# Fewer filling multiplications at the start of a linear attention and MLP kernel, low words of the weights on ScalarE, and a new order of its work

## The chip, the cores and the metric

The kernel runs on one core of one Trainium2 chip. The metric is the device time of one execution in microseconds (us). TensorE multiplies matrices into PSUM; VectorE, ScalarE and GpSimd work on elements; SyncE issues nearly all the transfers. Each engine takes its own instructions strictly in the order in which the program lists them.

## The reference

The first part is a recurrence over 768 time steps for 4 batches and 8 heads of dimension 48. Its output, 3072 tokens of 384 numbers, goes through an MLP with an ELU:

```python
for t in range(S):                       # S = 768
    cur = einsum('bhd,bhe->bhde', u * k[t], v[t])
    y[:, :, t] = einsum('bhd,bhde->bhe', r[t], state + cur)
    state = w[t][..., None] * state + einsum('bhd,bhe->bhde', k[t], v[t])
x = y as (3072, 384)
h = x @ w_in                             # 384 x 2048
g = where(h > 0, h, exp(min(h, 0)) - 1)
out = g @ w_out                          # 2048 x 384
```

Inputs are float32 but the two MLP weights, which come as float64.

## The kernel before

**Attention.** The sequence is cut into 6 stages of 128 steps, and each stage into 4 *units* (24 in all, numbered from 0). The first four units take one batch each with a chunk of 128 steps, the others two batches with a chunk of 64. A unit needs on VectorE two scans over the decays w (`es`, `gs`), a product of the hats with k and r (`rh`), and a mask (`mk`); on TensorE the scores (`s`, with the transposes of k) and the values and state update (`v`); on ScalarE copies out of PSUM (`kt`, `xf`, `xh`). The diagonal of the scores, with the bonus u, comes for units 0 to 3 from a product `rkc` on VectorE, four small matmuls `pd` on TensorE (line 475), a copy `md` and eight spreading copies `sp` on ScalarE (line 485). For later units GpSimd makes two products (`rk`, `rku`, lines 458 and 461) and VectorE or GpSimd spreads. The mask `mk` (line 540) needs both the scores and the spread diagonal, and `v` needs the mask.

**MLP.** A stage has 512 tokens and 16 steps, one for each 128 of the 2048 hidden columns: `g1` multiplies into `ph`, `r1`, `r2`, `stt` make the ELU, `g2` adds into three accumulators. In stage 0 the first six steps run in two halves of 256 tokens, the first half as soon as units 0 and 1 are done, with plain float32 weights (lines 259 and 291). Other steps split both factors into a high and a low part (`gh`, `gl`, `w_h`, `w_l`) and use three matmuls for each (lines 263 and 294).

**Weights.** Each of the 16 tiles of weights is loaded as raw 64-bit words (line 606, `raw`). It is turned into float32 by `a` on ScalarE (line 611, scaling the high words), `cs` (`conv_low`, shifting the low words: line 616 on ScalarE or 618 on VectorE, by the table `LOW`), and two VectorE passes `cb` and `cc` (lines 626 and 630). For the split, `wh` (line 633) rounds and `wl` (line 645) subtracts. There are four raw buffers at first and later two; a tile's buffer comes free with `cc`.

**Order.** A planner with a table of assumed durations (`COST`), buffer counts (`SLOTS`) and due times lists all tasks once for all engines. Among the ready tasks of an engine it takes the one with the smallest due time plus its entry in `NUDGE`, which is keyed by the kind of task and its number. `RAW_AT` gives the earliest time of the plan at which the raw tiles 0, and 1 and later, may be issued. Ahead of a task with an entry in `FILL` the emitted program has that many multiplications of a matrix of ones with itself, 128 x 128 in float32 (`warm`, line 410). Their product is never read. The plan doesn't know of them.

Of the kernel before, what the change touches and what calls it, by code (L numbers as in the profile page):

```python
# [38 lines left out]
CUT = 384  # L39
K32 = 6  # L40
SIGN_ACT = ()
LOW = ['DVE']*2+['ACT']*14
RAWS = ["raw0", "raw1", "x1a", "x1b"] * 2 + ["raw0", "raw1"] * 4
DUE = {0: 9.0}
FILL = {("pd", 0): 29, ("s", 0): 12, ("v", 0): 1, ("pd", 1): 5, ("v", 1): 2, ("pd", 2): 7, ("s", 2): 5, ("g1", 0): 12}


def _pieces():
    res = []
    for h in range(H):  # L50
        s, e = h * D, (h + 1) * D
        while s < e:
# [22 lines left out]
FIRST = "ACT"  # L75
SPARE = (1,)
PAD = 32
RAW_AT = (1.6, 4.0)
LEAD = 69.5
DIAG = ['PE']*4+['POOL']*20  # L80
SPREAD = ["ACT"] * 4 + ["DVE"] * 4 + ["POOL"] * 16
# [2 lines left out]

LEADS = dict(ld="ld_w ld_k ld_v ld_rk ld_wx", es="es gs", rh="rkc rh kh pc sc", sp="rk rku md pd sp", fl="fl", s="s mk kt", v="v xf xh xl up", raw="raw", a="a",
             cc="cand cs cb cc cx sg", wl="wh wl wt", g1="g1 r1 r2 stt", g2="g2 gh gl")
NUDGE = dict(cc={0: 5, 2: 19.5, 4: 15.75, 5: -13.25, 14: 4.25},
             es={3: 11.5, 5: -23.75, 7: 1, 11: -42.5, 17: -5.25, 20: 12.75, 21: 40.5},
             g1={16: -3.5, 19: -3.5, 20: 4.25, 23: 5.75, 29: -7.5, 30: -8.25, 31: -13.25, 33: 21, 38: -15.75, 40: -29.75, 42: -33.75, 44: -17.5, 48: -70.75, 51: 26.75, 55: 44, 56: -10.5, 58: -10, 68: 34, 82: -8, 83: 12.5, 84: 6, 93: -7.5},
             g2={2: 6.75, 3: 26.5, 10: 1.5, 19: -1.75, 25: 0.25, 27: 2.25, 30: 0.75, 31: 14.75, 32: -6.5, 35: 9, 37: -11.25, 43: 28.5, 46: -25.25, 51: 8.5, 58: -13, 64: 2.25, 65: 14.5, 71: -25.5, 85: 6.5, 93: 1.75},  # L90
             ld={2: -16, 13: -16.5, 21: -36.75},
             raw={0: -6.75, 1: -6},
             rh={1: 10.25, 4: -3.75, 9: -18.75, 14: 23.5, 16: -14},
             s={4: -29.75, 9: -2.25, 12: -30.25, 13: 5, 21: 8.5},
             sp={4: -19.25, 5: 8.75, 9: 39.5, 13: 29.5, 17: -6.5},
             v={2: -5.5, 15: -2, 17: 6.75, 18: 24, 20: 22.25})
KIND = {n: k for k, v in LEADS.items() for n in v.split()}


class Plan:  # L100
# [5 lines left out]
    def add(self, key, eng, dur, fn, after=(), due=None, start=0.0, lock=False, size=0):  # L106
        self.tasks[key] = dict(key=key, eng=eng, dur=dur, fn=fn, after=list(after), due=due, start=start, lock=lock, size=size,
                               nudge=NUDGE.get(KIND.get(key[0]), {}).get(key[1] if len(key) > 1 else 0, 0.0))

# [212 lines left out]
def rwkv_elu_kernel(ctx, tc, wkr, rk, vp, u, uz, gkrw, gv, gu, wraw, out):  # L322
# [84 lines left out]
    def warm(n):  # L407
        pw = spare()[2][:, 0:P]
        for _ in range(n):
            nc.tensor.matmul(pw, ones, ones, start=True, stop=True)  # L410
# [193 lines left out]
    def load_w(f):  # L604
        raws[f] = raw_tile(f), None
        nc.sync.dma_start(raws[f][0].rearrange("p i k c -> p (i k c)"), wraw[f].bitcast(U32))

    def conv_a(f):
        g = w_f[f].bitcast(U32) if f < K32 else stg.tile([P, 2, NK, P], U32, tag="wg", name="wg", bufs=SLOTS["wg"])
        raws[f] = raws[f][0], g  # L610
        act(g.bitcast(F32), raws[f][0][:, :, :, 1::2].bitcast(F32), AF.Copy, scale=2.0 ** -112)  # L611

    def conv_low(f):
        w0 = raws[f][0][:, :, :, 0::2]
        if LOW[f] == "ACT":
            act(w0, w0, AF.Copy, bias=7.5 * 2.0 ** -10 - 0.5, scale=2.0 ** -29 - 2.0 ** -39)
        else:
            nc.vector.tensor_scalar(out=w0, in0=w0, scalar1=29, scalar2=None, op0=ALU.logical_shift_right)
# [106 lines left out]
    for f in range(NF):  # L725
        add(("raw", f), "SP", DMA_ISSUE, lambda f=f: load_w(f), start=RAW_AT[min(f, 1)], size=694)
        add(("a", f), "ACT", K["a"], lambda f=f: conv_a(f), [("raw", f)])
        e = LOW[f]
        add(("cs", f), e, K["la" if e == "ACT" else "cand"], lambda f=f: conv_low(f), [("raw", f)], lock=e == "DVE")
# [105 lines left out]
    with tc.manual_schedule():  # L835
        for t in plan.order():
            warm(FILL.get(t["key"], 0))
            t["fn"]()
# [137 lines left out]
```

## Time and profile before

| | us |
|---|---|
| median of 3 runs | 518.42 |
| lowest and highest run | 518.3, 519.65 |
| the profiled execution's own time | 517.97 |
| its span, first to last instruction | 515.8 |
| busy in the span: TensorE | 506.8 (98%) |
| busy: VectorE | 335.4 (65%) |
| busy: ScalarE | 270.6 (52%) |
| busy: GpSimd | 97.1 (19%) |

In the profile PE is TensorE, PEld its weight loads, DVE VectorE, ACT ScalarE, POOL GpSimd and SP SyncE. L410 is line 410 of the kernel. Names such as `am<-upper,pa` are the tile written and the tiles read. Ends of matmuls are modelled, so neighbouring ones overlap in the rows and a busy TensorE need not be at its peak. A float32 matmul leaves two records.

### The profile page before, as it was taken

The numbers are of one execution on the slowest core, as the hardware profiler recorded it, in microseconds if no ns is written. First come the engines' busy times: TensorE is split into PE (matmuls) and PEld (weight loads), VectorE is DVE, ScalarE is ACT, GpSimd is POOL, SyncE is SP. The second block draws the span as 40 slices with busy tenths as digits, with TensorE's granted clock in tenths as the row PEclk, the third lists the DMA queues.
The fourth block names the chain that finished last, engine by engine and source line by source line (L and its number), as shares of the span: only waits on it lengthen the run. The fifth ranks groups of instructions, "written<-read, shape, count | busy, mean of one in ns | idle before, by whom it ended". The sixth has DMA issues, their size and how long they took to land.

```text
span 515.8 us, 13882 instructions
## 1 busy us (share of the span) xinstructions
PE 506.8 (98%) x6070; PEld 417.8 (81%) x6070; DVE 335.4 (65%) x469; ACT 270.6 (52%) x520; POOL 97.1 (19%) x94
## 2 busy tenths in 40 slices
PE   9999999999999999999999999999999999999995
PEld 9998787787888888888788888887888877888884
DVE  6789999999589643498743487842499642423242
ACT  2779667657655344565545564443545443535351
POOL 2000123103455100264100174400161100000000
PEclk9999999999999999999999999999999999999998
DMA  8936944600843000856200674202332000010001
GB/s 258 337 132 201 319 139 142 189 3 4 260 117 106 3 3 3 243 154 160 57 19 3 197 204 143 75 0 79 99 101 56 22 1 3 0 62 0 1 1 66
DMA packets 18882, 51.09 MB, mean 99 GB/s; under 512 B 2304, under 2 KB 2688, under 8 KB 18816
## 3 DMA queue, kind: packets, MB, share of 16 engines
q1 hardware_dynamic: 18672, 50.08, 32.0%
q8 instruction: 49, 0.80, 0.6%
q14 instruction: 17, 0.14, 0.1%
q10 hardware_dynamic: 144, 0.07, 0.0%
HBM read 45.42 MB, written 4.72 MB: 97 GB/s over the span
## 4 chain that ended last, share of the span: by engine, by line
PE 86%; DVE 5%; ACT 3%; DMA 2%; issue 2%; POOL 0%; DVEq 0%; ACTq 0%; SPq 0%; POOLq 0%
PE ph L263 33%; PE acc L294 33%; PE pa L503 6%; PE acc L410 4%; PE pa L528 3%; PE pa L568 2%; PE ph L259 2%; PE acc L291 2%; PE pb L516 1%; DMA wx<-in_wkr_dram 1%; DMA wraw<-in_wraw_dram 1%; DVE m L273 1%; ACT m L270 1%; DVE wg L626 1%; ACT wg L611 1%
## 5 line engine op out<-in xcount | busy, mean ns | idle before, releaser
L273 DVE SCALAR_TENSOR_TENSOR m<-m,ph 128x512 f32<-128x512 f32 (+1 forms) x102 | 66.3, 651 | 98.3 <-ACT m L270 98.0
L267 ACT ACTIVATE m<-ph 128x512 f32<-128x512 f32 (+1 forms) x102 | 58.2, 571 | 108.7 <-PE ph L263 97.0
L263 PE MATMUL ph<-xh,w_l 128*128 128x512 f32 x270 | 105.4, 390 | 0.0
L294 PE MATMUL acc<-gh,w_l 128*128 128x512 f32 x268 | 104.6, 390 | 0.0
L281 DVE TENSOR_TENSOR gl<-m,gh 128x512 fp32r<-128x512 f32 x90 | 65.2, 726 | 39.4 <-ACT gh L277 39.3
L277 ACT CAST gh<-m 128x512 fp32r<-128x512 f32 x90 | 55.7, 619 | 59.4 <-PE acc L294 30.5
L294 PE MATMUL acc<-gh,w_h 128*128 128x512 f32 x180 | 71.9, 399 | 0.0
L263 PE MATMUL ph<-xh,w_h 128*128 128x512 f32 x180 | 71.6, 398 | 0.1
L294 PE MATMUL acc<-gl,w_h 128*128 128x512 f32 x180 | 70.3, 390 | 0.0
L263 PE MATMUL ph<-xl,w_h 128*128 128x512 f32 x180 | 70.1, 390 | 0.0
L270 ACT ACTIVATE m<-m 128x512 f32<-128x512 f32 (+1 forms) x102 | 61.9, 607 | 2.2
L263 PEld LDWEIGHTS ph<-xh,w_l 128*128 128x128 f32 x270 | 50.7, 188 | 10.9
L294 PEld LDWEIGHTS acc<-gh,w_l 128*128 128x128 f32 x268 | 50.3, 188 | 10.7
L458 POOL TENSOR_TENSOR rk<-rk 128x384 f32<-128x384 f32 x20 | 28.3, 1416 | 121.2 <-DMA rk<-in_rk_dram 116.7
L496 POOL TENSOR_SCALAR_AFFINE_SELECT am<-md 64x512 f32<-64x512 f32 x32 | 29.1, 910 | 113.5 <-DVE md L465 56.3
L263 PEld LDWEIGHTS ph<-xh,w_h 128*128 128x128 f32 x180 | 33.8, 188 | 7.8 <-DVE m L273 0.5
L294 PEld LDWEIGHTS acc<-gh,w_h 128*128 128x128 f32 x180 | 33.8, 188 | 7.7
L294 PEld LDWEIGHTS acc<-gl,w_h 128*128 128x128 f32 x180 | 33.8, 188 | 6.8 <-DVE gl L281 0.2
L263 PEld LDWEIGHTS ph<-xl,w_h 128*128 128x128 f32 x180 | 33.8, 188 | 6.7
L263 PE MATMUL ph<-xh,w_g 128*128 128x512 f32 x90 | 36.3, 403 | 0.1
L263 PE MATMUL ph<-xl,w_g 128*128 128x512 f32 x90 | 35.1, 390 | 0.0
L294 PE MATMUL acc<-gh,w_g 128*128 128x512 f32 x88 | 34.8, 396 | 0.0
(116 smaller groups left out, 754.2 us busy)
## 6 DMA issues: line engine op xcount, KB each, us to landing
wraw<-in_wraw_dram SPq DMA_DIRECT2D x16, 768.0 KB, 5.4
k<-in_wkr_dram SPq DMA_DIRECT2D x24, 448.0 KB, 6.7
rk<-in_rk_dram SPq DMA_DIRECT2D x20, 384.0 KB, 4.2
v<-in_vp_dram SPq DMA_DIRECT2D x24, 256.0 KB, 6.8
w<-in_wkr_dram SPq DMA_DIRECT2D x24, 227.9 KB, 4.4
out_dram<-o SPq DMA_DIRECT2D x17, 256.0 KB, 2.1
wx<-in_wkr_dram SPq DMA_DIRECT2D x8, 227.9 KB, 2.9
ub<-in_u_dram SPq DMA_DIRECT2D x1, 192.0 KB, 4.5
```

The source lines that it names most:

```text
L263: nc.tensor.matmul(ph, w[f][:, 0, k], y[:, k], start=(k == n == 0), stop=(k == NK - 1 and n == 2))
L267: act(s["m"], s["ph"], AF.Relu, scale=-1.0)
L270: act(s["m"], s["m"], AF.Exp, scale=-1.0)
L273: stt_(s["m"], s["m"], -1.0, s["ph"], ALU.add, ALU.max)
L277: nc.scalar.copy(s["gh"], s["m"])
L281: nc.vector.tensor_tensor(s["gl"], s["m"], s["gh"].bitcast(F32), ALU.subtract)
L294: nc.tensor.matmul(a_, w[f][:, 1, m], fold(s, g[:, a:b]), start=(first and n == 0), stop=(final and n == 2))
L410: nc.tensor.matmul(pw, ones, ones, start=True, stop=True)
L458: eng.tensor_tensor(u_["rk"][:, 0], u_["rk"][:, 0], u_["rk"][:, 1], ALU.mult)
L496: nc.gpsimd.affine_select(out=am[rs].rearrange("t q p s -> t (q p) s"), in_=u_["md"][rs].rearrange("t q p -> t (q p)").unsqueeze(2).broadc ...
L503: nc.tensor.matmul(u_["py"][32 * j:32 * j + 32, h, k], l, r, **flags)
L528: nc.tensor.matmul(pa[1 - q][ts, p], u_["k"][rs, p, ts], u_["r"][rs, p, ts], start=True, stop=True)
```

## The change

The table `LOW` gives the low words of all 16 tiles to ScalarE; before, tiles 0 and 1 were shifted by VectorE. `FILL` loses 38 of its 73 multiplications and places the other 35 differently. `RAW_AT` lets tiles 1 and later be issued as early as tile 0. The whole table `NUDGE` is replaced, which changes the order of tasks on every engine and of the transfers. No function and no assumed duration changes.

```diff
-LOW = ['DVE']*2+['ACT']*14
+LOW = ['ACT']*16
...
-FILL = {("pd", 0): 29, ("s", 0): 12, ("v", 0): 1, ("pd", 1): 5, ("v", 1): 2, ("pd", 2): 7, ("s", 2): 5, ("g1", 0): 12}
+FILL = {("pd", 0): 15, ("s", 0): 6, ("pd", 1): 4, ("v", 1): 7, ("g1", 0): 3}
...
-RAW_AT = (1.6, 4.0)
+RAW_AT = (1.6,1.6)
...
-NUDGE = dict(cc={0: 5, 2: 19.5, 4: 15.75, 5: -13.25, 14: 4.25},
-             es={3: 11.5, 5: -23.75, 7: 1, 11: -42.5, 17: -5.25, 20: 12.75, 21: 40.5},
...
-             ld={2: -16, 13: -16.5, 21: -36.75},
-             raw={0: -6.75, 1: -6},
-             rh={1: 10.25, 4: -3.75, 9: -18.75, 14: 23.5, 16: -14},
-             s={4: -29.75, 9: -2.25, 12: -30.25, 13: 5, 21: 8.5},
-             sp={4: -19.25, 5: 8.75, 9: 39.5, 13: 29.5, 17: -6.5},
-             v={2: -5.5, 15: -2, 17: 6.75, 18: 24, 20: 22.25})
+NUDGE = dict(a={4: 7.75},
+             cc={1: -12.5, 3: -16.75, 5: 20.5},
+             es={3: 4.25, 5: -25.75, 7: 39, 8: 4.5, 12: 11, 14: 18, 17: 11.25},
...
+             ld={2: 12.25, 4: -9.75, 20: 7, 21: -9},
+             rh={4: 36.5, 6: 22.5, 9: 18, 10: -10.25, 16: -10.5, 20: -7.5},
+             s={5: 11, 12: 15.25, 18: 22},
+             sp={3: 4.75, 5: 5.5, 7: 36.5, 8: 9.75, 9: -23.75, 11: 49.25, 15: -1, 16: 10},
+             v={0: 11.75, 1: -10, 4: -2.25, 5: -9.75},
+             wl={12: 23.5, 14: 20.5, 15: 54.75})
```

## Rows read from the trace of the kernel before

**Rows 1.** Busy time of each engine by stretch, with the granted clock and DMA share

```profile
core 0: us, PE busy (x) PEld busy (x) DVE busy (x) ACT busy (x) POOL busy (x), PEclk, DMA share, GB/s
...
11.20:15.90 4.70, 4.70 (x49) 4.44 (x49) 0.02 (x2) 3.91 (x12) 0.00 (x0) 1.00 1.04 388
15.90:28.99 13.09, 13.09 (x187) 12.08 (x187) 12.11 (x17) 9.82 (x27) 0.00 (x0) 1.00 0.96 305
28.99:54.64 25.65, 25.65 (x234) 22.07 (x233) 23.54 (x33) 22.18 (x50) 2.07 (x3) 1.00 0.52 171
54.64:101.47 46.83, 45.04 (x440) 36.34 (x438) 45.19 (x60) 29.42 (x52) 10.41 (x7) 1.00 0.63 197
...
131.00:509.20 378.20, 378.05 (x4492) 308.37 (x4490) 216.77 (x305) 183.52 (x346) 75.89 (x65) 1.00 0.26 74
```

**Rows 2.** TensorE's waits, 28 to 510 us: sum, times, longest

```profile
PE pa L503 <- DVE am L542: 1.2, 1, 1.2
PE ph L259 <- DVE m L273: 0.3, 1, 0.3
PE acc L291 <- DVE m L273: 0.2, 1, 0.2
```

**Rows 3.** The chain of waits, its first pieces: start, length, what

```profile
1.07 9.63 PE acc L410 x58
10.70 0.79 PE pb L475 x8
11.49 2.79 PE acc L410 x24
...
15.75 1.31 PE acc L410 x10
...
18.18 1.01 PE pa L503 x32
...
28.99 2.59 PE ph L259 x12
```

**Rows 4.** VectorE's timeline to 29 us: start, length, in brackets the idle time before

```profile
6.33 0.67 DVE L470 TENSOR_TENSOR rkc<-k 112x512 f32<-112x512 f32 x1
...
8.06 1.20 DVE L451 TENSOR_TENSOR k<-k,eg 112x1024 f32<-112x1024 f32 x1
...
10.53 0.69 DVE L470 TENSOR_TENSOR rkc<-k 112x512 f32<-112x512 f32 x1
15.90 1.35 DVE L540 COPY_PREDICATED am<-upper,pa 128x512 f32<-128x512 uint32 x2 [4.68 <-PE pa L528]
...
28.64 0.96 DVE L626 SCALAR_TENSOR_TENSOR w_f<-w_f,wraw 128x768 uint32<-128x768 uint32 x1 [0.91 <-ACT wraw L616]
```

**Rows 5.** ScalarE's timeline, 11 to 18 us

```profile
11.53 0.17 ACT L479 COPY md<-pb 128x8 f32<-128x8 f32 x1 [6.31 <-PE pb L475]
...
11.79 2.45 ACT L485 ACTIVATE am<-ident,md 128x128 f32<-128x128 f32 x8
...
17.89 0.17 ACT L479 COPY md<-pb 128x8 f32<-128x8 f32 x1 [2.45 <-PE pb L475]
```

**Rows 6.** Matmuls on the ones to 6 us, and 6 to 11 us: shortest, median, longest

```profile
L410 PE MATMUL acc<-ones x23: 421/421/582, 1.1 to 5.9; 128*128 128x128 f32 x23
...
L410 PE MATMUL acc<-ones x37: 274/275/421, 5.7 to 10.4; 128*128 128x128 f32 x37
```

**Rows 7.** The two forms of the low words' shift: duration in ns

```profile
L618 DVE TENSOR_SCALAR wraw<-wraw x2: 553/556/559, 17.1 to 21.1; 128x768 uint32<-128x768 uint32 x2
...
L616 ACT ACTIVATE wraw<-wraw x14: 894/926/951, 27.7 to 103.2; 128x768 uint32<-128x768 uint32 x14
```

**Rows 8.** GpSimd's and VectorE's timeline, 53 to 54 us

```profile
53.22 1.00 POOL L458 TENSOR_TENSOR rk<-rk 128x384 f32<-128x384 f32 x1 [12.04 <-DMA rk<-in_rk_dram]
...
53.57 1.46 DVE L626 SCALAR_TENSOR_TENSOR wg<-wg,wraw 128x768 uint32<-128x768 uint32 x1 [0.47 <-ACT wg L611]
```

More of the change, by code (lines that the diff above doesn't have):

```diff
@@ L86 @@
              cc="cand cs cb cc cx sg", wl="wh wl wt", g1="g1 r1 r2 stt", g2="g2 gh gl")
-NUDGE = dict(cc={0: 5, 2: 19.5, 4: 15.75, 5: -13.25, 14: 4.25},
-             es={3: 11.5, 5: -23.75, 7: 1, 11: -42.5, 17: -5.25, 20: 12.75, 21: 40.5},
-             g1={16: -3.5, 19: -3.5, 20: 4.25, 23: 5.75, 29: -7.5, 30: -8.25, 31: -13.25, 33: 21, 38: -15.75, 40: -29.75, 42: -33.75, 44: -17.5, 48: -70.75, 51: 26.75, 55: 44, 56: -10.5, 58: -10, 68: 34, 82: -8, 83: 12.5, 84: 6, 93: -7.5},
-             g2={2: 6.75, 3: 26.5, 10: 1.5, 19: -1.75, 25: 0.25, 27: 2.25, 30: 0.75, 31: 14.75, 32: -6.5, 35: 9, 37: -11.25, 43: 28.5, 46: -25.25, 51: 8.5, 58: -13, 64: 2.25, 65: 14.5, 71: -25.5, 85: 6.5, 93: 1.75},
-             ld={2: -16, 13: -16.5, 21: -36.75},
-             raw={0: -6.75, 1: -6},
-             rh={1: 10.25, 4: -3.75, 9: -18.75, 14: 23.5, 16: -14},
-             s={4: -29.75, 9: -2.25, 12: -30.25, 13: 5, 21: 8.5},
-             sp={4: -19.25, 5: 8.75, 9: 39.5, 13: 29.5, 17: -6.5},
-             v={2: -5.5, 15: -2, 17: 6.75, 18: 24, 20: 22.25})
+NUDGE = dict(a={4: 7.75},
+             cc={1: -12.5, 3: -16.75, 5: 20.5},
+             es={3: 4.25, 5: -25.75, 7: 39, 8: 4.5, 12: 11, 14: 18, 17: 11.25},
+             g1={2: 6.5, 3: -3.5, 13: 9, 15: 28.25, 16: -7.75, 17: -11, 26: -52.25, 29: -21, 35: -30.75, 39: 21.25, 43: -6, 47: -20.75, 48: 53.75, 49: -9.25, 59: -17.5, 68: 20.25, 81: -6, 84: -15.25, 96: -3},
+             g2={1: -6.75, 5: 24, 10: 9, 14: 10.75, 17: 19.25, 25: 5, 30: 21.75, 35: 4.25, 39: -16, 50: -6, 59: 8.75, 63: 8.75, 69: -3.75, 83: 9.75, 87: -1.75, 89: 4.5},
+             ld={2: 12.25, 4: -9.75, 20: 7, 21: -9},
[4 more added lines that the diff above has]
+             wl={12: 23.5, 14: 20.5, 15: 54.75})
 KIND = {n: k for k, v in LEADS.items() for n in v.split()}
```

## Prediction

> **What bounds the kernel now.** I read the page's busy table first: TensorE is busy nearly all of the span and VectorE two thirds of it. An average over unlike stages says little, so I read busy time by stretch next [rows 1]. There the reader is to see three regimes. From 131 to 509.2 us TensorE has practically no gap while VectorE is busy 217 of 378 us: here TensorE's work alone sets the pace, and nothing that only frees VectorE can help. From 15.9 to 101.47 us both are nearly full: VectorE's three rows add up to 12.11 + 23.54 + 45.19 = 80.84 us of 85.57, TensorE's to 83.78 of 85.57. Before 15.9 us VectorE stands still for almost a whole stretch (0.02 of 4.70 us) while TensorE is full.
>
> The list of TensorE's waits from 28 to 510 us has three entries, 1.2, 0.3 and 0.2 us, all on VectorE and all before 102 us [rows 2]. So after the first MLP step at 28.99 us TensorE runs its list almost without a pause, and the end can move in three ways only: that step and what follows start earlier, the waits of 1.7 us go, or new waits arise. The tail behind 509.2 us (6.6 us of evacuation and output) is the same in both kernels.
>
> What fills TensorE before 28.99 us is read from the chain of waits [rows 3]: it goes through L410, the multiplications of a matrix of ones with itself. They compute nothing, but TensorE takes its instructions in order, so work behind them waits. The trace has two records for each: 58, 24, 24 are the 29, 12 and 12 of the table FILL. The VectorE and ScalarE timelines show what they hold up [rows 4, 5]: the product rkc of unit 0 is done at 7.00 us, but the matmuls pd that need it start at 10.70, behind 29 ones; hat products of unit 0 end at 9.26, but the scores start past 14 us, behind 12 more; so VectorE's mask at 15.90 has waited 4.68 us, released by TensorE's L528.
>
> **The change part by part.** *Fills.* 73 become 35; by place 29 to 15 ahead of pd 0, 12 to 6 ahead of s 0, 1 to 0 (v 0), 5 to 4 (pd 1), 2 to 7 (v 1), 7 and 5 to 0 (pd 2, s 2), 12 to 3 (g1 0): 38 fewer. At the full rate 24 records took 2.79 us [rows 3], 0.2325 us a multiplication; 38 of them are 8.8 us of TensorE. That is the most that their removal by itself can give.
>
> At the start they are slower: 23 records begin between 1.1 and 5.9 us, 4.8/22 = 0.218 us each, 0.44 a multiplication, and their duration is 421 ns against 275 later [rows 6]. The 29 took 9.63 us [rows 3]; n at 0.44 and the rest at 0.2325 gives n = 13.9, so the rate rose after about 6.1 us of them, near 7.2 us. Fifteen then take 13.9 x 0.44 + 1.1 x 0.2325 = 6.4 us and end at 7.45 us, just behind rkc 0 (7.00). pd 0 moves from 10.70 to about 7.5, 3.2 us earlier.
>
> The rest of unit 0 by the durations of before: pd 0.79, so to 8.3; the copy md and the eight ScalarE spreads, 11.53 to 14.24 before [rows 5], shift by 3.2 to end at 11.05. The six fills (1.4 us) end at 9.7, past the hats (9.26); transposes and scores (from the 24 fills' end at 14.28 to the next ones at 15.75: 1.47 us [rows 3]) end near 11.2. Both allow the mask at 11.35 us instead of 15.90. VectorE's rkc 1 ends at 11.22 [rows 4]: the idle 4.68 us shrinks to about 0.13, 4.55 us are won.
>
> Unit 1 likewise: mask 0 (1.35) and hats 1 (1.22) let TensorE do v 0 to 14.3 and s 1 to 15.9; sp 1 on ScalarE ends near 16; mask 1 near 17.3; v 1 near 19.2, its seven fills (1.6 us) in the gap of the mask; xf 1 at 19.7. The first MLP step could then start at about 20, 9 us earlier than 28.99, which agrees with the 8.8 us of TensorE.
>
> *Low words of tiles 0 and 1.* They go from VectorE (2 x 0.556 = 1.11 us off a full engine) to ScalarE (2 x 0.926 = 1.85 us on) [rows 7]. ScalarE sat idle 2.45 us before its copy at 17.89 [rows 5], and by the times above still has room for one of them before md 1 and for the other before xf 1; the cover is its waiting for TensorE. With cover gone it costs up to 1.85 us, since VectorE's L626 waits for the low words, with the VectorE queue behind it (0.91 us of such a wait stands in [rows 4]). Bounds 0 to 1.85; I take 0.2, near the covered end.
>
> *Load times.* Tiles 1 and later of the raw weights may be issued from 1.6 instead of 4.0 us. The DMA engines are full until 29 us (shares 1.04 and 0.96 in the two stretches from 11.2 us [rows 1]), so a tile ahead of unit 1's keys would delay them by its 0.79 MB (128 x 1536 words of 4 bytes) over the 305 GB/s of that stretch, an estimate of 2.6 us. Bounds 0 to 2.6. VectorE needs the keys at 10.53 us [rows 4], and unit 1 is off the binding engine's path while VectorE has conversions to do: I take 0.3.
>
> *Order.* The NUDGE table reorders every queue. Nothing of before prices it. On the gaining side stand VectorE's gaps from 15.9 to 101.47 us, 85.57 - 80.84 = 4.73 us [rows 1], and VectorE work that is stretched while GpSimd multiplies: L626 takes 1.46 us at 53.57 beside a product that began at 53.22, against 0.96 at 28.64 [rows 4, 8]. On the losing side stands a TensorE wait of any length. I take 0 and keep both for the range.
>
> **The sum.** VectorE is full once the mask has started, and must deliver all that TensorE eats until 101.47 us. It starts its block 4.55 us earlier and has 1.11 us less to do: 5.66 us. Less 0.2 and 0.3: 5.2 us. TensorE could give 8.8, so some 3 us of it return as TensorE waits on VectorE between 20 and 101 us. The profiled execution took 517.97 us (span 515.8), so 512.8; the median of before is 0.45 above it, and I forecast 513.0.
>
> **A rule against the change.** The row first: ones at 0.44 us until near 7.2 us and 0.2325 from there on [rows 3, 6], that is the lower and the upper of TensorE's two levels (1.2 and 2.4 GHz), after 6.1 us without a pause. The granted clock reads 1.00 throughout [rows 1], so durations are the better witness here. The Trainium skill, TensorE: Matmul & The Clock Gate, section Part 1: The HAM clock gate, says that the low level is the default, that sustained activity releases it and that idling brings it back. By that rule the thinner fills might leave the first units and MLP steps at 1.2 GHz; the rise shown agrees with it, no run here shows a fall. By the row alone the sum is 5.2 us; by the rule it would be the second rival's.
>
> **Rivals.**
> First, TensorE alone is the bound: the new order lets VectorE postpone work past 131 us, where it has 161 us free [rows 1]. Then all 8.8 us arrive: 509.2; with the 1.7 us of waits also gone, 507.5. Against it speaks that conversions and units are needed in the order in which TensorE eats them. Chance 0.17.
>
> Second, the clock: the rate does not hold, or rises late. Scores and values of units 0 and 1 (1.5 us for the scores, at least the 1.01 of L503 for the values [rows 3], an estimate of 1.5) take twice as long, about 6 us more before the first MLP step, which comes at 26 instead of 20; then another 6 us at half rate lose 3. That is 29 against 28.99: no gain, 517 to 519.5. For it: 15 fills end close to where the rate rose. Against: the rise came before they end, and what follows has gaps of one or two us only. Chance 0.15.
>
> Third, the other side: the new order opens a wait in the stretch past 101.47 us, where before has none [rows 2], so that nothing can absorb it. The place: the last weight tile, whose low part is put back by 54.75 in priority. If TensorE reaches its step before it, it stands for what is left of the conversion: two ScalarE and two VectorE passes, 2 x 0.93 + 2 x 0.96 = 3.8 us [rows 7, 8], then the rounding and the subtraction over the same tile, by the same rows another 1.9, so 5.7 us, and up to as much again if the tile before it is late too. It decides from 5.2 us on, and makes the kernel slower than can be mistaken from 6.8; at 8 us it gives 520.8. Against it: VectorE has 43% of its time free past 131 us [rows 1]. Chance 0.12.
>
> **How the numbers follow.** The forecast has 0.56, with its own range 510 to 516.5 (more of the VectorE gaps used, or the load and ScalarE bounds of 2.6 and 1.85 paid in part). A difference of 0.3%, 1.56 us, is about what a measurement of this kernel tells from none: faster ends at 516.9, slower begins at 520.0. Faster: 0.17 + 0.54 = 0.71; same: 0.02 of the forecast and most of the second rival, 0.16; slower: the third and a rest of the second, 0.13. The range leaves out most of the third and the lowest part of the first: 508.5 to 519.0.
>
> **What would show it.** In the changed profile: 70 records at L410; pd 0 at 7.5 us and VectorE's mask near 11.4 with no long wait; L618 gone and 16 records at L616; the first L259 at 20 to 23 us, and the ones ahead of it at 275 ns and not 421; then TensorE waits on VectorE or ScalarE of about 3 us in sum before 101 us; and none past it. The prediction is wrong if the mask of unit 0 still waits, if matmuls before 30 us run at the low level, if TensorE waits more than about 5 us between 20 and 100 us, or if a wait stands past 101 us.

## The result and the profile after

The changed kernel takes 513.07 us (median of 4 runs, 512.33 to 513.81) against 518.36 (4 runs, 517.35 to 519.65): ratio 0.9897, 95% interval 0.987 to 0.9923, so 5.3 us faster by the medians. 513.0 had been forecast. The profiled execution took 513.81 us with a span of 512.1, the slowest of its four, where that of before (517.97) was near the fast end of its runs; between these two executions the difference is 4.2 us.

First TensorE's timeline of the changed kernel to the first MLP step (start, length, what; lines are one higher than before), which answers to [rows 3]:

```profile
1.07 6.31 PE L411 MATMUL acc<-ones 128*128 128x128 f32 x30 [1.07 <-POOL ones L378]
7.30 1.05 PE L476 MATMUL pb<-ubd,rkc 112*128 112x2 f32 x8
8.22 1.58 PE L411 MATMUL acc<-ones 128*128 128x128 f32 x12
...
20.71 2.76 PE L260 MATMUL ph<-xf,w_f 128*128 128x256 f32 x12
```

The same view of the kernel before has

```profile
10.54 0.95 PE L475 MATMUL pb<-ubd,rkc 112*128 112x2 f32 x8
...
28.83 2.75 PE L259 MATMUL ph<-xf,w_f 128*128 128x256 f32 x12
```

So pd 0 starts at 7.30 us instead of 10.54, and the first MLP step at 20.71 instead of 28.83 (the chain in [rows 3] puts them at 10.70 and 28.99). VectorE's timeline, for [rows 4], has its first two masks here:

```profile
11.58 1.35 DVE L541 COPY_PREDICATED am<-upper,pa 128x512 f32<-128x512 uint32 x2
...
16.76 1.36 DVE L541 COPY_PREDICATED am<-upper,acc 128x512 f32<-128x512 uint32 x2 [0.86 <-PE acc L529]
```

The first comes at 11.58 us instead of 15.90, and the 4.68 us of idle time ahead of it are gone. What became of the 8.1 us that the first MLP step won is read from busy time by stretch, as in [rows 1]:

```profile
core 0: us, PE busy (x) PEld busy (x) DVE busy (x) ACT busy (x) POOL busy (x), PEclk, DMA share, GB/s
...
28.99:54.64 25.65, 24.43 (x220) 20.21 (x219) 24.80 (x36) 21.08 (x45) 4.09 (x3) 1.00 0.62 202
54.64:101.47 46.83, 44.72 (x557) 36.12 (x556) 45.94 (x62) 32.80 (x55) 11.17 (x7) 1.00 0.53 160
...
131.00:505.00 374.00, 373.14 (x4469) 304.23 (x4467) 211.01 (x303) 178.47 (x339) 66.09 (x62) 1.00 0.25 69
505.00:520.00 15.00, 0.00 (x1) 0.00 (x0) 0.33 (x2) 0.00 (x0) 0.00 (x0) 0.81 0.11 39
```

TensorE stands still for 1.22 + 2.11 = 3.33 us in the two stretches before 101.47 us, where it was 0 + 1.79 before, and for 0.86 us past 131, where it was 0.15. Its work ends at 505.00 us. Before, 4.77 us of it stood behind that time, so that it ended at 509.77:

```profile
505.00:520.00 15.00, 4.77 (x26) 3.90 (x24) 2.22 (x4) 1.69 (x3) 0.00 (x0) 0.80 0.16 57
```

The list of TensorE's waits (sum, times, longest) names them, as [rows 2] did:

```profile
PE ph L264 <- DVE m L274: 2.1, 3, 0.9
...
PE ph L260 <- DVE m L274: 0.9, 1, 0.9
PE pa L504 <- issue: 0.6, 1, 0.6
```

Most of it ends at L274, the VectorE step of the ELU. In sum TensorE waits 2.3 us more than before. The first MLP step won 8.1 us, and 1.1 us of ones ahead of s 2, behind that step, are gone too. The 2.3 us of waits come back of this, and 0.8 us because pd 2 stood ahead of that step before and now stands behind it. That leaves 6.1 us, but TensorE ends only 4.8 us earlier: in this execution the matmuls that are 512 wide take 0.9 us more in sum (396.4 against 395.5) and those of the values 0.6 more, which is about the rest. The two spans differ by less still, 3.7 us, because what follows TensorE's work took 7.1 us instead of 6.0. From the last issue of an output transfer to the end it is 5.7 us before, 6.7 here and 6.0 in the profile of the first experiment below, so a part of any difference between two single executions lies in this tail.

### The profile page after: what moved, and what is told of

Read it like the earlier page. It is cut to its first block, busy times and chain, and to the rows that moved or that the text cites. A ratio compares the mean times of both kernels' runs of the same rounds, so it can differ in the third digit from the quotient of the medians.

```text
span 512.1 us, 13733 instructions
## 1 busy us (share of the span) xinstructions
PE 499.7 (98%) x5994; PEld 409.8 (80%) x5994; DVE 330.1 (64%) x467; ACT 271.6 (53%) x522; POOL 94.4 (18%) x94
## 4 chain that ended last, share of the span: by engine, by line
PE 86%; DVE 8%; issue 3%; ACT 2%; POOL 0%; DVEq 0%; POOLq 0%
PE ph L264 35%; PE acc L295 35%; PE pa L504 6%; PE pa L529 3%; PE pa L569 2%; PE acc L411 2%; PE pb L517 1%; PE acc L292 1%; DVE k L452 1%; DVE eg L437 1%; DVE w_f L627 1%; PE ph L260 1%; DVE m L274 1%; DVE st L551 1%; DVE eg L447 1%
## 5 line engine op out<-in xcount | busy, mean ns | idle before, releaser
L274 DVE SCALAR_TENSOR_TENSOR m<-m,ph 128x512 f32<-128x512 f32 (+1 forms) x102 | 66.4, 652 | 98.5 <-ACT m L271 97.8
L264 PE MATMUL ph<-xh,w_l 128*128 128x512 f32 x270 | 105.5, 391 | 0.0
L282 DVE TENSOR_TENSOR gl<-m,gh 128x512 fp32r<-128x512 f32 x90 | 62.7, 698 | 44.2 <-ACT gh L278 43.9
L264 PE MATMUL ph<-xh,w_h 128*128 128x512 f32 x180 | 71.8, 399 | 1.6 <-DVE m L274 1.5
L264 PE MATMUL ph<-xl,w_h 128*128 128x512 f32 x180 | 70.3, 390 | 0.0
L264 PEld LDWEIGHTS ph<-xh,w_l 128*128 128x128 f32 x270 | 50.7, 188 | 10.8
L264 PEld LDWEIGHTS ph<-xh,w_h 128*128 128x128 f32 x180 | 33.8, 188 | 10.3 <-DVE m L274 2.8
L264 PEld LDWEIGHTS ph<-xl,w_h 128*128 128x128 f32 x180 | 33.8, 188 | 6.7
L264 PE MATMUL ph<-xh,w_g 128*128 128x512 f32 x90 | 36.4, 404 | 0.6 <-DVE m L274 0.6
L264 PE MATMUL ph<-xl,w_g 128*128 128x512 f32 x90 | 35.2, 391 | 0.0
```

The source lines that it names most:

```text
L264: nc.tensor.matmul(ph, w[f][:, 0, k], y[:, k], start=(k == n == 0), stop=(k == NK - 1 and n == 2))
L274: stt_(s["m"], s["m"], -1.0, s["ph"], ALU.add, ALU.max)
L282: nc.vector.tensor_tensor(s["gl"], s["m"], s["gh"].bitcast(F32), ALU.subtract)
```

## The experiments

Each ratio is to the kernel before, measured beside it on the same chip (its medians were 517.84 to 518.50 us), with its 95% interval. Where two changed kernels are compared with each other, their ratios are subtracted, half-widths are added in squares, and 0.001 is 0.52 us. Changing LOW or NUDGE makes the planner list the work anew; changing FILL leaves the lists as they were but for a few neighbours on ScalarE.

**FILL alone.** On the kernel before:

```diff
-FILL = {("pd", 0): 29, ("s", 0): 12, ("v", 0): 1, ("pd", 1): 5, ("v", 1): 2, ("pd", 2): 7, ("s", 2): 5, ("g1", 0): 12}
+FILL = {("pd", 0): 15, ("s", 0): 6, ("pd", 1): 4, ("v", 1): 7, ("g1", 0): 3}
```

> The kernel before with the new FILL table alone: the 35 multiplications, the old order, low words and load times. Theory (the fills held back the first mask, and VectorE's block starts earlier): mask 0 on VectorE at 11.4 to 11.8 us instead of 15.90, first MLP step at 20 to 23 us, time 513.8 to 515 (a gain of 3.5 to 4.5; VectorE keeps the 1.11 us of low words). Rival (the new order makes the gain): less than 1.5 us gained, 517 or more, the earlier start being lost again in TensorE waits before 101 us.

512.75 us, ratio 0.9915 (0.9889 to 0.9941): 4.4 us, against 5.3 of the whole change, and the two intervals overlap. The time lies a little under the theory's range, the gain at its upper end, since the kernel before took 517.84 us beside it. The mask is at 11.49 us, the first MLP step at 22.50. The fills make the gain.

**Everything but FILL.** On the changed kernel, without the 12 multiplications of the two places pd 2 and s 2:

```diff
-FILL = {("pd", 0): 15, ("s", 0): 6, ("pd", 1): 4, ("v", 1): 7, ("g1", 0): 3}
+FILL = {("pd", 0): 29, ("s", 0): 12, ("v", 0): 1, ("pd", 1): 5, ("v", 1): 2, ("g1", 0): 12}
```

> The changed kernel with the old counts ahead of pd 0, s 0, v 0, pd 1, v 1 and g1 0 (29, 12, 1, 5, 2, 12: 61 multiplications), order and low words as changed. Theory: mask 0 back near 15.8 us, first MLP step near 27, time 516.5 to 518. Rival (order): at most 514.5.

517.09 us, ratio 0.9988 (0.9968 to 1.0009): no gain is shown, though 12 multiplications fewer run than in the kernel before.

**The order alone, the low words alone, and each combination.** The second of these has only this edit on the kernel before; the first undoes it and FILL (as just shown) on the changed kernel:

```diff
-LOW = ['DVE']*2+['ACT']*14
+LOW = ['ACT']*16
```

> The new NUDGE and RAW_AT with the old LOW and the old counts of the first six places of FILL. Theory: between 517 and 519.5, no gain from the order by itself. Rival (order): 514.5 or less.

523.06 us, ratio 1.0107 (1.008 to 1.0134): slower by 5.5 us, outside what either theory said. It differs from everything but FILL in `LOW` alone (and in the lists that follow from it), by 6.2 us.

> The kernel before with the low words of tiles 0 and 1 on ScalarE and nothing else. Theory: VectorE has 1.11 us less to do and ScalarE's 1.85 us are covered, so 517.0 to 518.0, a gain of 0.4 to 1.1 us. Rival (ScalarE is the limit at the start): 518.5 to 520, with a longer wait of VectorE's L626 for ScalarE.

517.44 us, ratio 0.9999 (0.9971 to 1.0027): no gain shown. Two more complete the table: the changed kernel with the low words of tiles 0 and 1 back on VectorE, and the kernel before with the new FILL and LOW.

> The changed kernel with the low words of tiles 0 and 1 back on VectorE; since the planner knows which engine shifts, its order moves too. Theory by my sum (VectorE is full): 1.1 us over the changed kernel, 513.8 to 515. Rival (the new order only fits the new low words, as the slow run of the order by itself suggests): 516.5 to 520, most of the gain of the fills lost.

518.21 us, ratio 0.9989 (0.9968 to 1.0011). TensorE's waits in it:

```profile
PE pa L504 <- DVE am L543: 3.6, 4, 1.4
...
PE acc L292 <- DVE m L274: 1.0, 3, 0.5
PE ph L264 <- DVE m L274: 0.9, 1, 0.9
PE pb L517 <- ACT md L480: 0.8, 1, 0.8
```

The gain of the fills is lost. Over the whole profile TensorE's waits behind 20 us add up to 8.2 us against 4.2 in the changed kernel, the largest part for masks of later units that come late (L543). Another part is the clock, which fell for a few us although all 35 ones were there (third column from the end):

```profile
29.00:60.00 31.00, 28.44 (x229) 23.29 (x228) 29.49 (x40) 25.38 (x51) 3.49 (x4) 0.94 0.63 197
```

The matmuls in it, scores at 32.18 us and a step of the MLP at 33.92, take 1.81 and 3.82 us instead of 1.16 and 2.75. This profile is the slowest of the twelve executions, so the two parts need not have these sizes in the others.

> The kernel before with the new FILL and the new LOW, the old NUDGE and RAW_AT. Theory by my sum: 1.1 us under the run of FILL alone, 511.8 to 513.2, as good as the changed kernel or better. Rival (the low words give nothing by themselves, as measured alone): 512.8 to 514.5.

513.53 us, ratio 0.9905 (0.9871 to 0.994), beside 0.9915 without the new LOW and 0.9897 with the new order too: no difference shown among the three. So the new order is worth nothing measurable with the low words on ScalarE, and with two of them on VectorE it costs 5.5 and 3.8 us (1.0107 against 1; 0.9989 against 0.9915). It fits the new LOW only. In its profile this kernel has the same 35 ones as the changed one, and yet the granted clock (third column from the end) fell, after TensorE had waited 0.92 us for ScalarE:

```profile
16.00:22.00 6.00, 5.08 (x60) 0.78 1.03 323
```

With FILL alone the same wait stands there and the column reads 1.00.

**Which fills?** On the kernel before, first only the 20 that go ahead of the first mask are taken out, then only the 24 behind the work that leads to the first two masks:

```diff
+FILL = {("pd", 0): 15, ("s", 0): 6, ("v", 0): 1, ("pd", 1): 5, ("v", 1): 2, ("pd", 2): 7, ("s", 2): 5, ("g1", 0): 12}   # early
+FILL = {("pd", 0): 29, ("s", 0): 12, ("v", 0): 1, ("pd", 1): 5, ("v", 1): 2}                                              # late
```

> The kernel before with 15 and 6 instead of 29 and 12 ahead of pd 0 and s 0, the other places of FILL as before: 20 multiplications fewer, 4.65 us of TensorE, all of them ahead of the first mask. Theory (VectorE's start sets the gain): mask 0 at 11.4 to 11.8 us, 513.5 to 515, as much as the whole new FILL or nearly. Rival (it is TensorE's time alone): in proportion to the 38, 515 to 516.

515.46 us, ratio 0.9942 (0.992 to 0.9964): 3.0 us (1.9 to 4.1) of the 4.65 removed. The mask is at 11.30 us.

> The kernel before with 29, 12, 1, 5, 2 as before but nothing ahead of pd 2, s 2 and g1 0: 24 multiplications fewer, 5.6 us of TensorE, none of them ahead of the first two masks. Theory (VectorE's start sets the gain): mask 0 stays near 15 to 16 us, the first MLP step comes 2 to 4 us earlier, and TensorE waits for VectorE instead: 517 to 518.5, a gain under 1 us. Rival (TensorE's time): 512.5 to 514.

514.74 us, ratio 0.9934 (0.9909 to 0.9959): 3.4 us (2.1 to 4.7) of the 5.6 removed, where my theory allowed less than 1. VectorE's first mask in it is as late as in the other profiles with 29 ones at the start (14.62 to 15.90 us), the first MLP step is not:

```profile
14.62 1.34 DVE L540 COPY_PREDICATED am<-upper,pa 128x512 f32<-128x512 uint32 x2 [3.61 <-PE pa L528]
```

```profile
21.75 1.20 PE L410 MATMUL acc<-ones 128*128 128x128 f32 x4
22.88 1.94 PE L503 MATMUL acc<-am,v 128*32 128x128 f32 x32
...
25.42 2.86 PE L259 MATMUL ph<-xf,w_f 128*128 128x256 f32 x12
```

The first two of these rows took 0.69 and 1.08 us before. Here, too, the granted clock fell (third column from the end), and these two rows lost 1.4 us by it of what had been removed; whether it fell in the other seven executions no profile shows:

```profile
22.00:29.00 7.00, 6.28 (x64) 0.79 0.79 270
```

These two falsify the step that VectorE alone sets the pace once its block has begun. By that step the first should have given nearly everything and the second next to nothing; they gave some 65% and 60% of TensorE's removed time, with wide intervals (40 to 90%, 40 to 85%), and of the second a part went to the clock.

**What a microsecond of each engine is worth.** The same question put to the changed kernel as doses: four idle reductions on VectorE behind the first four masks, or 19 more ones on TensorE behind what leads to the first two masks.

```diff
-    big.tile([P, PAD], F32, name="pad")
+    pad = big.tile([P, PAD], F32, name="pad")
...
-                nc.vector.copy_predicated(u_["am"][:, q], above[u_["L"]][:, q], u_["pa"][q])
+                nc.vector.copy_predicated(u_["am"][:, q], above[u_["L"]][:, q], u_["pa"][q]); q and nc.vector.tensor_reduce(pad[:, 0:8], ones.unsqueeze(1).broadcast_to([P, 8, P]), AX.X, ALU.add)
...
-FILL = {("pd", 0): 15, ("s", 0): 6, ("pd", 1): 4, ("v", 1): 7, ("g1", 0): 3}
+FILL = {("pd", 0): 15, ("s", 0): 6, ("pd", 1): 4, ("v", 1): 7, ("g1", 0): 3, ("g1", 2): 19}
```

> The changed kernel with four idle reductions on VectorE over 1024 elements each, one behind the mask of each of units 0 to 3, some 4.4 to 4.8 us of VectorE between 13 and 42 us; every list else as changed. If VectorE is full and sets the pace until 101 us, as my sum had it, nearly all of it arrives: 517 to 518.5. If TensorE's time sets it and VectorE has slack while it waits, under half: 513 to 515.3.

> The changed kernel with 19 more multiplications of the ones, 4.4 us of TensorE, between the second and third of the first MLP steps (near 24 us), behind all that leads to the first two masks. If VectorE alone sets the pace until 101 us, TensorE's waits of 3 to 4 us absorb most: 513 to 514.5. If TensorE's time sets it: 516 to 517.5.

The doses as they ran: in the first kernel the reductions (shortest, median, longest in ns; first and last start), in the second TensorE's timeline:

```profile
L541 DVE TENSOR_REDUCE pad<-ones x4: 1190/1206/1214, 12.6 to 43.2; 128x8 f32<-128x1024 f32 x4
```

```profile
24.00 4.49 PE L411 MATMUL acc<-ones 128*128 128x128 f32 x38
28.32 1.46 PE L260 MATMUL ph<-xf,w_f 128*128 128x256 f32 x6
```

4 x 1.206 = 4.8 us on VectorE gave 515.89 us, ratio 0.9952 (0.9933 to 0.9971), which is 0.0055 +- 0.0033 over the changed kernel: 2.9 us (1.2 to 4.5), some 60%. On TensorE the next step moved from 24.12 to 28.32, 4.2 us; it gave 516.31 us, ratio 0.9956 (0.9937 to 0.9976), 0.0059 +- 0.0033 over it: 3.1 us (1.4 to 4.8), some 70%. In the profiles TensorE's waits behind 20 us grow from 4.2 to 6.0 us with the dose on VectorE and shrink to 2.9 with the dose on TensorE: the one becomes waiting in part, the other is taken up by waits in part. Neither engine is free. VectorE's dose does not arrive whole (its interval ends at 94%); that TensorE's would, its interval does not exclude.

**Do the fills do anything?** On the changed kernel FILL is emptied, or only the first 15 are kept:

```diff
-FILL = {("pd", 0): 15, ("s", 0): 6, ("pd", 1): 4, ("v", 1): 7, ("g1", 0): 3}
+FILL = {}                  # the first kernel
+FILL = {("pd", 0): 15}     # the second
```

> The changed kernel with an empty FILL, no multiplication of the ones at all; order and low words as changed. Theory (TensorE's rate rises only after it has worked, and what comes first pays for it): pd 0 still near 7.3 us, since rkc 0 sets it; scores and values of units 0 and 1 at up to twice their time, mask 0 at 12.5 to 13.5 instead of 11.58 us, the first MLP records near twice their spacing for a while; time 514 to 517, 1 to 4 us over the changed kernel. Rival (the ones only cost): 512 to 513.5, and no record of the first units longer than now.

515.53 us, ratio 0.9953 (0.993 to 0.9976): 2.9 us over the changed kernel (1.1 to 4.7). TensorE's timeline:

```profile
6.93 1.86 PE L476 MATMUL pb<-ubd,rkc 112*128 112x2 f32 x8 [6.93 <-DVE rkc L471]
...
18.40 2.08 PE L529 MATMUL acc<-k 48*128 48x128 f32 x16
...
24.88 3.89 PE L260 MATMUL ph<-xf,w_f 128*128 128x256 f32 x12
28.61 0.95 PE L476 MATMUL pb<-ubd,rkc 112*128 112x2 f32 x8
```

pd takes 1.86 us at first and 0.95 from 28.6 us on: the work up to the first MLP step runs at the low level.

> The changed kernel with the 15 multiplications ahead of pd 0 alone (20 fewer). Theory: the rate has risen by the end of the 15 or soon after, the later 20 stand in gaps in which TensorE waits for the mask and the spread anyway: 512.3 to 513.8, the same as the changed kernel. Rival (the gaps of one or two us bring the rate down): 514.5 to 517, with first MLP records at twice their spacing.

515.57 us, ratio 0.9945 (0.9919 to 0.997): 2.5 us over the changed kernel (0.6 to 4.4), by the rival. TensorE's timeline, then its busy time and granted clock by stretch:

```profile
7.04 1.05 PE L476 MATMUL pb<-ubd,rkc 112*128 112x2 f32 x8 [0.41 <-DVE rkc L471]
9.51 0.57 PE L517 MATMUL pb<-ident,k 112*128 112x112 f32 x4 [1.41 <-DVE k L452]
10.01 1.16 PE L529 MATMUL pa<-k 48*128 48x128 f32 x16
12.09 1.86 PE L476 MATMUL pb<-ubd,rkc 112*128 112x2 f32 x8 [0.92 <-ACT kt L547]
...
24.18 3.57 PE L260 MATMUL ph<-xf,w_f 128*128 128x256 f32 x12
```

```profile
10.00:16.00 6.00, 5.08 (x63) 0.67 1.03 418
16.00:22.00 6.00, 4.49 (x52) 0.50 1.04 293
22.00:29.00 7.00, 7.00 (x63) 0.74 0.92 328
```

Here the scores of unit 0 still run at the high level (1.16 us, as with all the fills). After gaps of 0.41, 1.41 and 0.92 us it falls to 0.50, the lower of the two levels (1.2 and 2.4 GHz), and the first MLP step comes at 24.18 us instead of 20.71. All twelve executions have a mean granted clock of 0.980 to 0.989, the four of the changed kernel 0.997 or 0.998. The 15 alone are not told from none at all (0.9945 against 0.9953). With the 20 small ones behind them the level holds until the MLP begins in the changed kernel; as seen above, the same 35 did not hold it in two profiles with another LOW or another order.

## Why the prediction was right

*The fills, early.* As worked out: pd 0 at 7.30 us (7.5), the mask at 11.58 (11.4), the first MLP step at 20.71 (20 to 23), 70 records of the ones. The sum had 4.55 us for this; FILL alone measured 4.4. But the 4.55 came from an execution in which the rate rose late: the same 29 ones took 9.63 us in it and 8.35 to 8.98 in the four experiments that begin with the same 29 (all but FILL, order alone, low words alone, late fills alone), where the first mask starts at 14.62 to 15.24 us and VectorE has idled 3.4 to 3.8 us ahead of it. By the means of these five profiles and of the eight that begin with 15 (11.22 to 11.58 us) the mask came 3.7 us earlier.

*VectorE sets the pace.* This step failed, though the total held. "VectorE is full once the mask has started, and must deliver all that TensorE eats until 101.47 us" is contradicted by the late fills (3.4 us without an earlier mask) and by the doses: of VectorE's time some 60% arrives at the end, of TensorE's some 70%. Nearly all of VectorE's 4.73 us of gaps in [rows 1] are waits for ScalarE, and the longest group among them is for an input of the ELU, which ScalarE makes from what TensorE has just multiplied:

```profile
DVE m L273 <- ACT m L270: 2.1, 4, 1.1
DVE w_f L626 <- ACT wraw L616: 1.3, 2, 0.9
```

So each engine's delay can be passed on through the other, which fits what the doses gave; the way of each microsecond was not traced. A sum by that measure, 8.8 us of TensorE at 60 to 70%, is 5.3 to 6.2 us; that is the first rival's mechanism, at less than its full price, and a fit after the fact. That 513.0 stands so close to 513.07 is therefore in good part luck: the sum took the gain of an earlier mask from a late execution and counted it as the whole, while TensorE's removed time gave its share beside it.

*Low words.* Mis-sized: 1.11 us off VectorE less 0.2 was to give 0.9. Alone they measured 0.05 us (1.5 faster to 1.4 slower), on top of the new FILL 0.5 us with an interval of more than 2 on either side. At the 60% of the dose 1.1 us would give 0.7, which these runs can't tell from nothing.

*Load times and order.* The load times (0.3 us) were changed in no run without the order, so no run shows that term by itself. Unit 1's keys, which the prediction feared for, did not hold VectorE up: `rkc` of unit 1 starts at 9.43 us in the profile after, without a wait, against 10.53 before. The order was taken at 0. By itself, within the new FILL and LOW, it is not told from 0 (0.9897 against 0.9905). That it costs 3.8 to 5.5 us without the new LOW had not been thought of.

*The waits.* TensorE's waits of about 3 us before 101 us were forecast, 3.33 us stand there. "None past it" is wrong, and by the prediction's own signs such a wait was to show the prediction wrong: 0.86 us of idle time stand past 131 us. The third rival had it at the late weight tiles. The waits named there are for the ELU (L264, 0.6 us) and for nothing that the profile shows (0.3), and FILL alone (0.4) and the low words alone (0.9), with the old order, have a wait past 102 us as well. The tail, called the same in both kernels, was 1.1 us longer in the profile after.

*The clock.* The second rival did not occur in the changed kernel, whose profile reads 1.00 to the end of TensorE's work, but it is no idle threat. The two kernels with 15 ones and none pay for the low level, 2.5 and 2.9 us, and shorter falls stand in the profiles of three others (late fills, low words back on VectorE, FILL and LOW). The Trainium skill, TensorE: Matmul & The Clock Gate, section Part 1: The HAM clock gate, has idling bring the low level back. The run with 15 ones agrees in kind, though TensorE was not idle there for longer than 1.41 us at a time before the level fell. What the change did was to remove ones that TensorE's work waited for and keep enough to hold the level in the executions measured here.

No version was found that beats the changed kernel: the kernel before with the new FILL alone, and with FILL and LOW, are not told from it.

## What to carry to other kernels

Work that is there only to keep an engine warm is worth having in its idle gaps, and ahead of anything that is ready it holds that back by its full time (of which 60 to 70% reached the end here): compare its end with the moment when the next real input is ready, and cut to that. Then look at the granted clock again, in more than one execution. Where two engines are both 95% busy, don't book a saving on one as the whole gain; put a known dose of idle work on each and read what share arrives. An order that goes with one placement of work should not be judged, or kept, without that placement.

## What was not expected of the hardware

The granted clock in the profile doesn't show the low level at the start of an execution. With no ones at all the matmuls before the first MLP step take about twice their time (pd 1.86 us against 0.95 later, scores 2.08 against 1.16), and yet these stretches of that kernel (TensorE's busy time, granted clock, DMA share, GB/s) read 1.00:

```profile
10.00:16.00 6.00, 5.60 (x54) 1.00 1.02 415
16.00:22.00 6.00, 4.49 (x49) 1.00 1.05 275
```

In the kernel with 15 ones, where the level rose and fell again, the same column reads 0.50 over matmuls of the same lengths. So the length of a known matmul is the witness until a first change has been recorded. The level also fell there though TensorE had worked in between and no gap until then was longer than 1.41 us. And the same ones do not give the same clock each time: the first 15 took from 4.97 to 6.31 us in the eight profiles that begin with them, and behind the same 35 and the same wait of 0.92 us the level held with FILL alone and fell with FILL and LOW.
